# Pooling q by TensorE accumulation in the first batch of an attention and MoE kernel

## The chip, the cores and the metric

The kernel runs on one core of one Trainium2 chip. A core has five engines that work side by side, each on its own stream of instructions: TensorE (PE: matrix products; PEld in the profile is its loading of the stationary operand), VectorE (DVE), ScalarE (ACT), GpSimd (POOL) and SyncE (SP), which here only issues transfers between the main memory and the core's own memory. The metric is the time of one execution on the device, in microseconds (us); less is better.

## The reference

The inputs are q, k and v with 8 batches, 8 heads, 576 tokens and 64 numbers per head, and the weights of a MoE-like layer. Cut to what matters:

```python
q_d = q.reshape(B, H, Sd, 4, D).mean(axis=3)      # Sd = 576 / 4 = 144, k_d and v_d likewise
out_up = np.repeat(sm_attn(q_d, k_d, v_d), 4, axis=2)
scores = np.where(mask, scale * np.matmul(q, k.transpose(0, 1, 3, 2)), -1e9)   # |i - j| < 4
attn_out = out_up + np.matmul(softmax(scores), v)
h = x @ w_in                                       # x: attn_out as 4608 x 512; w_in: 512 x 2048
g = (a0 + a1*h + a2*h**2 + a3*h**3) / (1 + |b0|*|h| + |b1|*h**2 + 1e-6)
return g @ w_out                                   # w_out: 2048 x 512
```

Each head thus has two attentions: a local one in a band of 7 tokens, and a pooled one in which groups of four tokens have been averaged in q, k and v. The pooled scores are 144 x 144 for each head.

## The kernel before

**Pairs.** Two heads form a pair (class `Pair`), one head on the partitions 0 to 63 and one on 64 to 127 (j = 0 and 1). A batch has four pairs. A pair has a slot (class `Slot`) with its tiles: `qk` holds q and k for both heads, 64 numbers along the partitions, tokens along the rows (`s.qk.ap[:, 0]` is q, `[:, 1]` is k, each with 3 columns of padding ahead); `pq` holds the pooled q (`[:, 0]`) and pooled k (`[:, 1]`), 144 columns each. Batch 0 has four slots of its own, two of which lie in memory that weights need later; the later batches share slots 0 and 1.

**One pair's work.** `scores` (L427) forms the local scores in ten windows, after a mask has been put down (L417). `softmax_local` takes maxima on VectorE (L459), scales them (L466), and exponentiates on ScalarE (L474), with an accumulator read for the sums behind each exponential. `pool_qk` (L405) sums groups of four tokens of q and k on VectorE. `scores_pooled` (L444) forms the pooled scores for two pairs at a time: for each of NQ = 3 row blocks of 64 rows (blocks start 48 apart), each pair and each j one product, with 64 columns of pooled q as the stationary operand and the 144 columns of pooled k streaming. The output position alternates with the pair (`c.pos(j)`), so that the four products of a row block fall on the four different 64 x 64 quarters of the array. `softmax_pooled` takes the maxima (L489), scales them (L494) and exponentiates (L500). `normalize` (L511 to L535), `turned` (transposes L548 and L555, copies L561 to L572), `weighted_pooled` (L594) and `weighted_local` (L582), and `put_x` (L623) finish the pair into x.

**Batch 0** is the loop near L857: pairs 0 and 1 form its first group, pairs 2 and 3 its second. It runs before any MoE work can begin. There q and k are loaded once and pooled on VectorE. For the other batches `load_pooled` lets transfers that add in the memory (issued by GpSimd, L394) do the pooling, `pool_qk` is not called, and the pooled tiles come ready.

**The MoE part** goes over blocks of 512 rows of x. `h_part` forms h: the first block in plain fp32 (L718), the others in three products of split parts (L730). `middle` computes g on ScalarE (L743) and VectorE (L758 to L776), `o_part` forms the output (L795). The weights come as fp32 words and are split on ScalarE and VectorE (L338 to L361) while the first batch and block run. Batch 1 is computed beside the first block, and so on.

**The order.** Every step is given to `plan.add` with an engine, an estimated duration in us, what it reads and what it writes. `Plan.run` simulates the engines with these durations, takes at each moment the ready task with the earliest due time, and so fixes one order for each engine; the instructions are issued in that order and each engine goes through its own without overtaking. Where the plan leaves TensorE idle ahead of the first MoE work, `warm` puts in small dummy products (L929), in number 0.6 of the planned gap divided by 0.107 us. Waits between engines follow from what tasks read and write.

Of the kernel before, what the change touches and what calls it, by code (L numbers as in the profile page):

```python
# [14 lines left out]
ALU = mybir.AluOpType  # L15
AX = mybir.AxisListType.X

B, H, S, D = 8, 8, 576, 64
# [6 lines left out]
POOL = 4  # L25
SD = S // POOL
KC = SD // 2
NQ, QC = 3, SD // 3
# [5 lines left out]
PADL = 3  # L34
# [42 lines left out]
class Plan:  # L77
# [11 lines left out]
    def add(self, engine, dur, fn, reads=(), writes=(), due=None, lag=None):  # L89
        t = Task()  # L90
        t.engine, t.dur, t.fn, t.due, t.n = engine, dur, fn, due, len(self.tasks)
        t.lag, t.preds, t.succs, t.late, t.start = lag, {}, [], 1e9, None
        rk = set().union(*(r.keys for r in reads)) if reads else set()
        wk = set().union(*(w.keys for w in writes)) if writes else set()
        for k in rk | wk:
            w = self.writer.get(k)
            if w is not None:
                t.preds[w] = True
        for k in wk:
            for r in self.readers.get(k, ()):  # L100
                t.preds.setdefault(r, False)
            self.writer[k] = t
            self.readers[k] = []
        for k in rk - wk:
            self.readers[k].append(t) if k in self.readers else self.readers.__setitem__(k, [t])
        t.preds.pop(t, None)
        for p in t.preds:
            p.succs.append(t)
        self.tasks.append(t)
        return t  # L110
# [75 lines left out]
def attention_moe(  # L186
# [12 lines left out]
    nc = tc.nc  # L199
# [3 lines left out]
    add = plan.add  # L203
# [5 lines left out]
    def put(name, shape, dtype, at=None):  # L209
        nonlocal top  # L210
        offset = top if at is None else at
        n = 2 if dtype == BF16 else 4
        for d in shape[1:]:
            n *= d
        if at is None:
            top = -(-(offset + n) // 32) * 32
        ap = nc.alloc_sbuf_tensor_at(name, shape, dtype, offset=offset).ap()
        room = Room(ap, (("S", k) for k in range(offset // 32, -(-(offset + n) // 32))))
        room.at = offset
        room.size = n  # L220
        return room
# [7 lines left out]
    def flat(t):  # L229
        return t.rearrange("p a b -> p (a b)")  # L230

    high, low, bits = [], [], [[], []]
    for name, parts in (("wh", high), ("wl", low)):
        for w in range(2):
            parts.append([])
            for f in range(NFC):
                t = put(f"{name}{w}_{f}", [P, NCC, P], F32R)
# [159 lines left out]
                    (dst,), (dst,), lag=4.0,  # L397
                )

    def pool_qk(c):  # L400
        s = c.slot
        groups = s.qk.ap[:, :, PADL : PADL + S].rearrange("p t (s r) -> p t s r", r=POOL)
        add(
            "DVE", 1.28,
            lambda: nc.vector.tensor_reduce(out=s.pq.ap, in_=groups, axis=AX, op=ALU.add),  # L405
            (s.qk,), (s.pq,),
        )

    def scores(c, bk):

        s = c.slot

        def issue():
            for g in range(2):
                for j in range(2):
                    js = slice(j * D, (j + 1) * D)
                    nc.tensor.matmul(  # L417
                        bk[j].ap[g * D : (g + 1) * D, : NW // 2 * D],
                        lhsT=identb.ap[js, js], rhs=maskb.ap[js, g, :],
                        start=True, stop=False, skip_group_check=True,  # L420
                    )
            for w in range(0, NW, 2):
                for j in range(2):
                    js = slice(j * D, (j + 1) * D)
                    for g in range(2):
                        o = (w + g) * WQ
                        nc.tensor.matmul(  # L427
                            bk[j].ap[g * D : (g + 1) * D, w // 2 * D : (w // 2 + 1) * D],
                            lhsT=s.qk.ap[js, 0, PADL + o : PADL + o + D],
                            rhs=s.qk.ap[js, 1, o : o + D],  # L430
                            start=False, stop=True, skip_group_check=True,
                        )

        add("PE", 1.0, issue, (s.qk, identb, maskb), bk)

    def scores_pooled(cs, bk):
        def issue():
            for i in range(NQ):
                for c, x in zip(cs, bk):
                    pq = flat(c.slot.pq.ap)  # L440
                    for j in range(2):
                        js = slice(j * D, (j + 1) * D)
                        o = c.pos(j) * D
                        nc.tensor.matmul(  # L444
                            x.ap[o : o + D, i * SD : (i + 1) * SD],
                            lhsT=pq[js, i * QC : i * QC + D],
                            rhs=pq[js, SD:],
                            start=True, stop=True, skip_group_check=True,
                        )

        add("PE", 0.9, issue, [c.slot.pq for c in cs], bk)

    def softmax_local(c, bk):
        s = c.slot
        nm, sm = s.nm.ap, s.sm.ap
        view = two(bk)[:, :, : NW // 2 * D].rearrange("p j (c k) -> p j c k", k=D)
        add(
            "DVE", 0.74,
            lambda: nc.vector.tensor_reduce(  # L459
                out=nm[:, :NW].rearrange("p (j c) -> p j c", j=2), in_=view, axis=AX, op=ALU.max, negate=True  # L460
            ),
            bk, (s.nm,),
        )
        add(
            "DVE", 0.115,
            lambda: nc.vector.tensor_tensor(  # L466
                out=nm[:, :NW], in0=nm[:, :NW], in1=scales.ap[:, :NW], op=ALU.mult
            ),
            (s.nm, scales), (s.nm,),
        )  # L470

        def exps(j):
            for k in range(NW // 2):
                nc.scalar.activation(  # L474
                    out=s.el.ap[:, k, c.pos(j), :], in_=view[:, j, k, :], func=AF.Exp,
                    bias=nm[:, 5 * j + k : 5 * j + k + 1], scale=scale,
                    accum_out=sm[:, 2 * k + c.pos(j) : 2 * k + c.pos(j) + 1],
                )

        for j in range(2):  # L480
            add("ACT", 1.45, lambda j=j: exps(j), (bk[j], s.nm), (s.el, s.sm))

    def softmax_pooled(c, x):
        s = c.slot
        nm, sm = s.nm.ap[:, NW:13], s.sm.ap
        view = x.ap[:, : NQ * SD].rearrange("p (c k) -> p c k", k=SD)
        add(
            "DVE", 0.52,
            lambda: nc.vector.tensor_reduce(out=nm, in_=view, axis=AX, op=ALU.max, negate=True),  # L489
            (x,), (s.nm,),  # L490
        )
        add(
            "DVE", 0.115,
            lambda: nc.vector.tensor_tensor(out=nm, in0=nm, in1=scales.ap[:, NW:13], op=ALU.mult),  # L494
            (s.nm, scales), (s.nm,),
        )

        def exps():
            for i in range(NQ):
                nc.scalar.activation(  # L500
                    out=s.ep.ap[:, i, :], in_=view[:, i, :], func=AF.Exp,
                    bias=nm[:, i : i + 1], scale=scale / 16.0,
                    accum_out=sm[:, NW + i : NW + i + 1],
                )

        add("ACT", 1.07, exps, (x, s.nm), (s.ep, s.sm))
# [125 lines left out]
    def weighted_pooled(c, y):  # L632

        add("PE", 1.1, lambda: pooled_sums(c, y), (c.slot.ept, *vf), (y,))
        keep_up(c, y)
# [219 lines left out]
    bk = banks  # L855
    for q in range(2):
        cs = c0[2 * q : 2 * q + 2]  # L857
        for i, c in enumerate(cs):
            scores(c, bk[2 * i : 2 * i + 2])
            softmax_local(c, bk[2 * i : 2 * i + 2])  # L860
        for c in cs:
            pool_qk(c)
        sp = bk[4:6] if q == 0 else bk[0:2]
        scores_pooled(cs, sp)
        for c, y in zip(cs, sp):
            softmax_pooled(c, y)
        for i, c in enumerate(cs):
            normalize(c)
            (tp, t0, t1), (x, y) = FIRST[2 * q + i]
            turned(c, [bk[tp], bk[t0], bk[t1]])  # L870
            weighted_pooled(c, bk[y])
            weighted_local(c, bk[x], bk[y], due0 - 10.0 * (1 - q))
# [26 lines left out]
    for n in range(NS + LAG):  # L899
        if n < NS:  # L900
            k, s = steps[n]
# [8 lines left out]
        o = n - LAG  # L910
        if o >= 0:
            k, s = steps[o]
# [21 lines left out]
    for t in pe:  # L934
        n = int(WARM * (t.start - end) / 0.107)
# [88 lines left out]
```

## Time and profile before

| | us |
|---|---|
| three runs, median (lowest to highest) | 976.98 (975.13 to 977.01) |
| the profiled execution | 976.34 |
| its span, first to last instruction | 974.5 |
| TensorE busy in the span | 961.0 |
| VectorE busy | 833.1 |
| ScalarE busy | 810.5 |
| GpSimd busy | 147.4 |

A row of the profile names a line of the kernel, the engine and operation, the tile written and the tiles read, the shapes, and how often it occurred (x24). An engine is called busy while an instruction of it is open; TensorE's products overlap each other, so that the sum of their durations exceeds the time they took together. An entry in square brackets is the idle time of the engine just before, and what ended it. Stage tables give the same by stretches of time, counted from the start of the span. The granted clock is the share of TensorE's full clock that it was allowed. The DMA share is the mean busy share of the 16 transfer engines.

### The profile page before, as it was taken

To read this page: it belongs to the slowest core of one execution; us is meant where nothing else is said; L and a number is where in the kernel's file an instruction comes from. 1 tells how busy PE (TensorE), PEld (TensorE's weight loads), DVE (VectorE), ACT (ScalarE), POOL (GpSimd) and SP (SyncE) were. 2 spreads that over 40 slices of the span, in tenths; PEclk is the share of its full clock that TensorE was granted. 3 is DMA by queue.
4 is the path that set the end of the run, shared out by engine and by line. 5 is a ranking of instruction groups with operands and counts; after the bars stand their busy time and mean duration, and the time that the engine had idled before them with its cause. 6 is when DMAs were issued, how large, how long until landed. Compare 5 with 4: busy or idle time off the path is not lost.

```text
span 974.5 us, 19826 instructions
## 1 busy us (share of the span) xinstructions
PE 961.0 (99%) x7389; PEld 759.9 (78%) x7389; DVE 833.1 (85%) x1472; ACT 810.5 (83%) x2078; POOL 147.4 (15%) x176
## 2 busy tenths in 40 slices
PE   7999999999999999999999999999999999999997
PEld 5666657887887879987878878878788887998885
DVE  6899999998878888878788787878887888888886
ACT  6899998988789887679787979788988988867775
POOL 1121312030302121002221121203130220000000
PEclk9999999999999999999999999999999999999999
DMA  9974644252423342014333343324242320100001
GB/s 314 311 236 143 155 127 99 77 89 69 83 94 56 96 73 73 1 48 75 83 75 90 80 75 85 85 76 90 72 85 82 69 49 2 44 1 23 1 1 43
DMA packets 46359, 83.43 MB, mean 86 GB/s; under 512 B 6552, under 2 KB 29080, under 8 KB 46264
## 3 DMA queue, kind: packets, MB, share of 16 engines
q1 hardware_dynamic: 25912, 63.00, 19.6%
q0 software_dynamic: 20352, 19.19, 14.2%
q8 instruction: 58, 0.95, 0.4%
q14 instruction: 37, 0.30, 0.1%
HBM read 72.72 MB, written 9.44 MB: 84 GB/s over the span
## 4 chain that ended last, share of the span: by engine, by line
PE 86%; DVE 6%; ACT 4%; DMA 2%; issue 1%; ACTq 0%; SPq 0%; DVEq 0%
PE psum L795 38%; PE psum L730 37%; PE psum L582 3%; DMA qk<-in_qk_dram 2%; PE psum L594 2%; PE psum L548 2%; PE psum L555 2%; ACT m L743 2%; PE psum L427 1%; PE psum L444 1%; ACT el L474 1%; PE psum L718 1%; DVE m L770 1%; DVE g L767 1%; PE psum L417 1%
## 5 line engine op out<-in xcount | busy, mean ns | idle before, releaser
L795 PE MATMUL psum<-wh,g 128*128 128x512 f32 x1152 | 371.0, 403 | 0.8 <-DVE g L776 0.8
L730 PE MATMUL psum<-xs,wh 128*128 128x512 f32 (+1 forms) x1152 | 263.6, 367 | 0.0
L743 ACT ACTIVATE m<-psum,cf 128x512 f32<-128x512 f32 x288 | 215.4, 753 | 44.9 <-PE psum L730 43.3
L795 PEld LDWEIGHTS psum<-wh,g 128*128 128x128 f32 x1152 | 208.6, 188 | 50.6 <-issue 5.5
L730 PEld LDWEIGHTS psum<-xs,wh 128*128 128x128 f32 x1152 | 201.1, 188 | 37.6 <-ACT gb L743 1.0
L795 PE MATMUL psum<-wl,g 128*128 128x512 f32 x576 | 224.8, 391 | 0.0
L743 ACT ACTIVATE gb<-psum,cf 128x512 f32<-128x512 f32 x144 | 115.0, 799 | 57.5 <-PE psum L795 57.5
L767 DVE TENSOR_TENSOR g<-m,m 128x512 fp32r<-128x512 f32 x144 | 99.2, 689 | 57.1 <-ACT m L743 54.7
L394 POOL DMA_DIRECT2D pq<-in_qkp_dram x84 | 74.4, 929 | 478.2 <-DMA pq<-in_qkp_dram 436.2
L730 PE MATMUL psum<-xs,wl 128*128 128x512 f32 (+1 forms) x576 | 143.8, 371 | 0.0
L795 PEld LDWEIGHTS psum<-wl,g 128*128 128x128 f32 x576 | 108.3, 188 | 23.9
L764 DVE TENSOR_TENSOR m<-m,gb 128x512 f32<-128x512 f32 x144 | 99.0, 687 | 28.4 <-ACT gb L743 25.3
L730 PEld LDWEIGHTS psum<-xs,wl 128*128 128x128 f32 x576 | 99.6, 189 | 16.8
L474 ACT ACTIVATE el<-psum,nm 128x64 f32<-128x64 f32 x320 | 96.7, 346 | 16.0 <-DVE nm L466 16.0
L758 DVE SCALAR_TENSOR_TENSOR m<-m,cf,m 128x512 f32<-128x512 f32 x144 | 107.4, 746 | 0.3 <-ACT m L743 0.2
L743 ACT ACTIVATE gb<-m,cf 128x512 f32<-128x512 f32 x144 | 106.6, 740 | 1.1 <-DVE m L758 1.1
L770 DVE SCALAR_TENSOR_TENSOR m<-m,g 128x512 f32<-128x512 f32 x144 | 99.3, 690 | 3.1
L775 DVE TENSOR_TENSOR m<-m,m 128x512 f32<-128x512 f32 x144 | 99.2, 689 | 2.2
L776 DVE TENSOR_TENSOR g<-m,m 128x512 fp32r<-128x512 f32 x144 | 98.3, 683 | 0.8
L763 DVE TENSOR_TENSOR m<-m,m 128x512 f32<-128x512 f32 x144 | 98.5, 684 | 0.0
L743 ACT ACTIVATE m<-gb 128x512 f32<-128x512 f32 x144 | 93.5, 649 | 5.1 <-DVE m L763 2.7
L394 POOL DMA_DIRECT2D vp<-in_vp_dram x84 | 71.8, 902 | 156.2 <-DMA vp<-in_vp_dram 148.4
(63 smaller groups left out, 987.9 us busy)
## 6 DMA issues: line engine op xcount, KB each, us to landing
qk<-in_qk_dram SPq DMA_DIRECT2D x32, 590.0 KB
pq<-in_qkp_dram POOLq DMA_DIRECT2D x84, 144.0 KB, 3.4
vw<-in_vw_dram SPq DMA_DIRECT2D x32, 320.0 KB
out_dram<-xf SPq DMA_DIRECT2D x32, 256.0 KB
vp<-in_vp_dram POOLq DMA_DIRECT2D x84, 72.0 KB, 2.9
sx<-in_w_in_dram SPq DMA_DIRECT2D x11, 512.0 KB
sx<-in_w_out_dram SPq DMA_DIRECT2D x11, 512.0 KB
pq<-in_qkp_dram SPq DMA_DIRECT2D x28, 144.0 KB
```

What stands on the lines that cost most here:

```text
L394: lambda d=dst, x=src, r=r: nc.gpsimd.dma_start(out=d.ap, in_=x[b, r, :, i], accum_op=ALU.add),
L474: nc.scalar.activation(out=s.el.ap[:, k, c.pos(j), :], in_=view[:, j, k, :], func=AF.Exp, bias=nm[:, 5 * j + k : 5 * j + k + 1], scale=sca ...
L730: nc.tensor.matmul(ph.ap[:, f * t : (f + 1) * t], lhsT=(high, low)[j][0][fc].ap[:, c, :], rhs=blk.x[i].ap[:, c, :], start=(part_ == 0 and ...
L743: add("ACT", cost, lambda: nc.scalar.activation(out=out_.ap, in_=in_, func=func, **kw), (room_in, cf, *more), (out_,))
L758: lambda: v.scalar_tensor_tensor(out=tb.ap, in0=tq.ap, scalar=b1, in1=tb.ap, op0=ALU.mult, op1=ALU.add),
L763: add("DVE", 0.61, lambda: v.tensor_tensor(out=ta.ap, in0=ta.ap, in1=tq.ap, op=ALU.mult), (ta, tq), (ta,))
L764: add("DVE", 0.61, lambda: v.tensor_tensor(out=ta.ap, in0=ta.ap, in1=u.ap, op=ALU.add), (ta, u), (ta,))
L767: add("DVE", 0.61, lambda: v.tensor_tensor(out=gh.ap, in0=ta.ap, in1=tq.ap, op=ALU.mult), (ta, tq), (gh,))
L770: lambda: v.scalar_tensor_tensor(out=tb.ap, in0=tb.ap, scalar=CONE, in1=gh.ap.bitcast(F32), op0=ALU.add, op1=ALU.mult),
L775: add("DVE", 0.61, lambda: v.tensor_tensor(out=tb.ap, in0=ta.ap, in1=tb.ap, op=ALU.subtract), (ta, tb), (tb,))
L776: add("DVE", 0.61, lambda: v.tensor_tensor(out=gl.ap, in0=tb.ap, in1=tq.ap, op=ALU.mult), (tb, tq), (gl,))
L795: nc.tensor.matmul(ob[sub].ap, lhsT=g[i].ap[:, f0 : f0 + P], rhs=flat((high, low)[j][1][fc].ap), start=(fc == 0 and m == 0), stop=(fc == N ...
```

## The change

In batch 0 VectorE sums groups of four of k alone; the step is renamed `pool_k`, and its planned duration goes from 1.28 to 0.68 us. The pooled q is no longer formed. `scores_pooled` takes q as it is: for a row block it reads, as four stationary operands, the columns of q at every fourth token, starting at the first, second, third and fourth of the group, multiplies each with the pooled k, and adds the four products in the same accumulator (start at the first, stop at the last). The innermost loop runs over these four, so that all four of one quarter follow each other before the next quarter's. For batch 0 the planned duration goes from 0.9 to 3.6 us, and the step now also reads the slots' `qk`. The other batches issue what they issued before.

```diff
-    def pool_qk(c):
+    def pool_k(c):
         s = c.slot
-        groups = s.qk.ap[:, :, PADL : PADL + S].rearrange("p t (s r) -> p t s r", r=POOL)
-        add(
-            "DVE", 1.28,
-            lambda: nc.vector.tensor_reduce(out=s.pq.ap, in_=groups, axis=AX, op=ALU.add),
+        groups = s.qk.ap[:, 1, PADL : PADL + S].rearrange("p (s r) -> p s r", r=POOL)
+        add(
+            "DVE", 0.68,
+            lambda: nc.vector.tensor_reduce(out=s.pq.ap[:, 1, :], in_=groups, axis=AX, op=ALU.add),
             (s.qk,), (s.pq,),
         )
...
                         o = c.pos(j) * D
-                        nc.tensor.matmul(
-                            x.ap[o : o + D, i * SD : (i + 1) * SD],
-                            lhsT=pq[js, i * QC : i * QC + D],
-                            rhs=pq[js, SD:],
-                            start=True, stop=True, skip_group_check=True,
-                        )
-
-        add("PE", 0.9, issue, [c.slot.pq for c in cs], bk)
+
+                        if c.b == 0:
+                            at = [PADL + POOL * i * QC + r for r in range(POOL)]
+                            ls = [flat(c.slot.qk.ap)[js, a : a + POOL * (D - 1) + 1 : POOL] for a in at]
+                        else:
+                            ls = [pq[js, i * QC : i * QC + D]]
+                        for n, l in enumerate(ls):
+                            nc.tensor.matmul(
+                                x.ap[o : o + D, i * SD : (i + 1) * SD],
+                                lhsT=l,
+                                rhs=pq[js, SD:],
+                                start=(n == 0), stop=(n == len(ls) - 1), skip_group_check=True,
+                            )
+
+        add("PE", 3.6 if cs[0].b == 0 else 0.9, issue, [c.slot.pq for c in cs] + [c.slot.qk for c in cs if c.b == 0], bk)
...
         for c in cs:
-            pool_qk(c)
+            pool_k(c)
```

## The prediction, made before the changed kernel ran

> **What bounds the kernel now.** I read the table of stages first (stretch, length, busy time of PE, weight loads, VectorE, ScalarE and GpSimd with instruction counts, granted clock, DMA share, GB/s).
>
> ```profile
> 0.00:10.00 10.00, 6.93 (x83) 5.14 (x83) 2.67 (x6) 1.74 (x4) 2.28 (x8) 1.00 0.80 242
> 10.00:20.00 10.00, 7.94 (x160) 5.51 (x160) 8.50 (x17) 10.00 (x66) 0.23 (x1) 1.00 1.04 348
> 20.00:30.00 10.00, 8.74 (x143) 6.69 (x137) 8.93 (x21) 9.46 (x49) 0.00 (x0) 1.00 1.03 399
> 60.00:80.00 20.00, 20.00 (x70) 12.92 (x70) 19.76 (x35) 19.94 (x43) 2.53 (x3) 1.00 0.51 145
> 140.00:160.00 20.00, 18.32 (x163) 13.18 (x162) 18.89 (x38) 17.93 (x43) 7.60 (x9) 0.91 0.50 80
> 300.00:900.00 600.00, 600.00 (x4638) 492.69 (x4637) 505.30 (x883) 498.86 (x1252) 92.44 (x108) 1.00 0.29 64
> ```
>
> The reader is to see three regimes. From 300 us on TensorE never rests, so the end is set by when that dense work begins. Between 60 and 80 us TensorE, VectorE and ScalarE are all full. Only the first 30 us have holes, and the change lies there. TensorE is idle for 1.68 us once more, between 140 and 160 us, at a clock of 0.91.
>
> Then the chain that ended last, in order of time (start, length, what), where it crosses batch 0:
>
> ```profile
> 19.76 0.95 DVE pq L405
> ...
> 25.76 1.10 ACT ep L500 x6
> ...
> 28.12 0.74 PE psum L548 x6
> ...
> 41.38 1.72 PE psum L718 x4
> ```
>
> The last of the four qk loads has landed and its pooling begins at 19.76. VectorE, then ScalarE carry the chain to 28.12; from there TensorE does, through the first MoE products (L718). So the question is: **does the change move the 28.12?** A shift there moves the first MoE step, and with it VectorE and ScalarE, which are full behind it; the 1.68 us of TensorE rest near 150 cannot swallow that, because those two are late as well.
>
> **The change part by part.** First VectorE, its reductions in the timeline (start, length, engine and line, out<-in with shapes, idle time before):
>
> ```profile
> 10.31 1.35 DVE L405 TENSOR_REDUCE pq<-qk 128x288 f32<-128x1152 f32 x1 [0.87 <-DMA qk<-in_qk_dram]
> 11.58 0.81 DVE L459 TENSOR_REDUCE nm<-psum 128x10 f32<-128x640 f32 x1
> ...
> 21.03 0.81 DVE L459 TENSOR_REDUCE nm<-psum 128x10 f32<-128x640 f32 x1
> ...
> 23.50 0.60 DVE L489 TENSOR_REDUCE nm<-psum 128x3 f32<-128x432 f32 x1
> ```
>
> 1152 elements take 1.35 us and 640 take 0.81, so 1.05 ns an element; 576 elements come to 0.81 - 64 x 0.00105 = 0.74 us. Each of the four poolings loses 0.6 us, 2.4 us together, and the next instruction can start 0.08 us before its end (10.31 + 1.35 against 11.58). Almost all of it falls into VectorE's own holes: in the first 20 us it is busy 11.17. The saved time is worth something only where a reduction is waited for.
>
> Now TensorE. [...]
>
> ```profile
> 7.56 0.75 PE L427 MATMUL psum<-qk 64*64 64x64 f32 x40
> ...
> 10.33 0.81 PE L427 MATMUL psum<-qk 64*64 64x64 f32 x40
> ...
> 11.40 1.28 PE L444 MATMUL psum<-pq 64*64 64x144 f32 x24
> ...
> 13.90 0.81 PE L427 MATMUL psum<-qk 64*64 64x64 f32 x40 [0.21 <-DMA qk<-in_qk_dram]
> ...
> 19.78 0.81 PE L427 MATMUL psum<-qk 64*64 64x64 f32 x40 [0.60 <-DMA qk<-in_qk_dram]
> 20.52 0.50 PE L929 MATMUL psum<-maskb,identb 128*128 128x256 bf16 x3
> 20.96 1.26 PE L444 MATMUL psum<-pq 64*64 64x144 f32 x24
> 22.15 0.48 PE L548 MATMUL psum<-ident,ep 112*72 112x112 f32 x3
> 22.46 2.24 PE L929 MATMUL psum<-maskb,identb 128*128 128x256 bf16 x19
> 24.63 0.71 PE L594 MATMUL psum<-ept,vf 72*64 72x144 f32 x8
> 25.81 0.71 PE L594 MATMUL psum<-ept,vf 72*64 72x144 f32 x8 [0.47 <-ACT ept L561]
> 26.45 0.33 PE L555 MATMUL psum<-ident,el 128*128 128x128 f32 x1
> ```
>
> The source issues 12 products in each L444 group and the row counts 24: an fp32 product is two passes. A pass of 512 columns takes 1.72 / 4 = 0.43 us (L718, chain above), 0.84 ns a column; so 144 columns take 0.121 us and 64 columns 0.054 us. The new group has 48 products, 96 passes. Each works on one quarter of the array (64*64; the quarter follows from j and from the pair), and a quarter gets 24 passes.
>
> How far the quarters run beside each other is the unknown that decides. L427 answers for the old order, where the quarter changes after every product: 40 passes in a row would be 2.15 us; were each product's second pass to hold up the next product, still 20 x 0.054 = 1.08; the row shows 0.75, and a record of one pass (0.054 of streaming) lasts about 0.22, most of it its way through the array. Less that 0.22, the starts spread over 0.53 us: 10 passes, just one quarter's share. So a pass that waits for its own quarter does not hold the other three. In the new order **a quarter gets 8 passes in a row** before the next one comes, and no row has a run longer than 2. Bounds for a group: all four quarters together, 24 x 0.121 = 2.9, and 0.4 for start and end (the 1.28 row has 0.55 beside its 6 x 0.121, a wait for the second pooling among it), 3.3 us; one pass at a time, 96 x 0.121 = 11.6 + 0.4 = 12 us. L427 is the nearest row (same kind of tile, same passes), so I take **3.3 us**. Between them lies a look-ahead that ends early: overlap of two quarters, 48 x 0.121 + 0.4 = 6.2 us. That the stationary operand is now read at every fourth element appears in no row; a load that still fits under a 0.121 us pass costs nothing, one four times as long as the pass it hides in would put the group at the 12 us end again, so the bounds hold it.
>
> [...]
>
> First group, at 3.3 us. Both poolings of k are done by 10.31 + 0.74 - 0.08 = 10.97 and the second pair's scores by 11.14; the products run 11.1 to 14.4, over idle-time matmuls. The third pair's scores move from 13.90 to 14.4 and end at 15.2; its L459 follows. ScalarE hides that:
>
> ```profile
> 15.51 0.43 ACT L474 ACTIVATE el<-psum,nm 128x64 f32<-128x64 f32 x1
> ...
> 22.14 0.31 ACT L474 ACTIVATE el<-psum,nm 128x64 f32<-128x64 f32 x1 [0.33 <-DVE nm L466]
> ...
> 25.61 0.42 ACT L500 ACTIVATE ep<-psum,nm 128x144 f32<-128x144 f32 x1
> ```
>
> It was full from 10 to 20 us; it did the first pair's pooled exponentials before the second pair's last five local ones at 15.51. (Such a set takes the 1.10 us of the chain: three exponentials and three reads of their sums.) Swapped, the local ones end near 15.51 + 0.4 = 15.9, and the pooled maxima are ready at 15.2 (14.4, one L489 of 0.60, 0.2 for the scaling and the waits). Cover left: 0.7 us, so the group may take 4.0. A longer one leaves ScalarE idle.
>
> Second group. The pooling frees VectorE at 20.4 instead of 21.03, the scores at 20.59, and with 0.1 us allowed for the signal L459 starts at 20.69 instead of 21.03, **0.34 us earlier**. ScalarE's L474 moves to 21.80 and would reach L500 at 25.27 instead of 25.61. L500 also needs the pooled products: 20.6 + 3.3 = 23.9, then an L489 for each pair and the scaling, so 24.7 for the first, 25.4 for the second (ScalarE asks for that at 26.3). Cover 0.5 us, so 3.8 us a group cost nothing and 4.1 still reach the old 25.61. What TensorE did between 22.15 and 28 that is not idle time is 0.48, two of 0.71 and 0.33 (their ends overlap the next), and it fits into 23.9 to 27.8. So 28.12 becomes about 27.8.
>
> The added reads of qk hold each slot until the products end, 14.4 instead of about 11.6 in the first group; the next load into a slot is for batch 1, whose scores stand behind the first MoE products of the chain (41.38), and the DMA share is already 1.04 and 1.03 there. I cost it at nothing; it would cost when that load became the last to land. The planner counts 3.6 and 0.68 us and reorders what follows; with the three engines full later on I cost the order at 0, between -1.5 and +1.5.
>
> **Sum:** -0.34 us, rounded -0.3, on the profiled execution's 976.34 (span 974.5 and 1.8 around it): 976.0. That execution lies 0.64 under the median of 976.98, so I forecast 976.7.
>
> **The rivals.**
>
> *Look-ahead ends early* (6.2 us a group). For it: no run of 8 in the profile. Against: L427. First group 11.1 to 17.3; pooled maxima at 18.1 leave ScalarE 2.2 us idle; the third pair's exponentials and the transposes of the first pair move by about 2, the fourth pair's scores to some 22.5, the second group to 23.3 to 29.5, L500 from 25.61 to 30.3. Of these 4.7 us TensorE can use at most 1 for waiting transposes: 980.5 to 982. It decides from about 4.1 us a group: below that the gain still covers it, at 5 us it costs some 1.5.
>
> *One pass at a time* (12 us). First group to 23.1, fourth pair's scores near 28.5, second group 29.3 to 41.3, L500 at 42.1, 16 us late: 993. Against it: the 0.75 us row, where passes on other quarters do overtake. [...]
>
> *VectorE's time is used after all.* It is full at 60 to 80 us, and the stage from 140 to 160 has 1.68 us of rest and 0.09 x 20 = 1.8 us of lost clock. If the planner pulls weight conversions into the freed 2.4 us, that stage closes earlier by 2 to 3: 974 to 975. Against: VectorE has holes there already, so it lacks data, not time.
>
> *The change does nothing*: 977.0, inside the forecast's own range of 975.5 to 977.8.
>
> **How the numbers follow.** Forecast (with "nothing") 0.53, early look-ahead 0.24, one pass at a time 0.05, VectorE's time used 0.18. A measurement of this kernel can tell about 0.2%, 1.95 us, from no change, so faster means under 975.0, slower over 978.9. Faster: 0.15 of the last case and 0.03 of the forecast. Slower: 0.16 of the early look-ahead (group above some 5.2 us), 0.05, and 0.05 of the forecast by the reordering: 0.26. Same: 0.56. The range runs from 974.0 to 982.0; it leaves out the 12 us case and the far ends of the others.
>
> **What would show it.** L444 as two groups of 96 passes, each 3.1 to 3.6 us from first to last; L405 near 740 ns; fewer L929; L459 of the fourth pair near 20.7; L500 of the third pair near 25.3; the first L548 of six near 27.8. Wrong if L444's groups last over 4.2 us, if ScalarE shows an idle stretch before L500 ended by VectorE's L494, or if the stage at 140 to 160 us changes its rest or clock.

## The result, and the profile after

| us | before | after |
|---|---|---|
| runs side by side, median (lowest to highest) | 976.73 (975.13 to 977.01, 4 runs) | 982.42 (981.62 to 982.98, 4 runs) |
| ratio with its 95% interval | | 1.0061 [1.0049, 1.0073] |
| the profiled execution | 976.34 | 982.98 |
| its span | 974.5 | 981.2 |

The changed kernel is 5.7 us slower, well past the 0.2% that can be told from no change. The forecast of 976.7 fell, and the time lies 0.4 us above the upper end of the range.

The stage table of the profile after (start and end, length, then busy time with instruction counts of PE, weight loads, VectorE, ScalarE and GpSimd, granted clock, DMA share, GB/s):

```profile
0.00:10.00 10.00, 6.95 (x79) 5.07 (x79) 2.24 (x7) 1.52 (x3) 2.51 (x8) 1.00 0.82 254
10.00:20.00 10.00, 10.00 (x192) 9.78 (x191) 5.25 (x10) 8.04 (x48) 0.00 (x0) 1.00 1.04 345
20.00:30.00 10.00, 10.00 (x151) 9.37 (x151) 6.21 (x16) 8.75 (x50) 0.00 (x0) 1.00 0.99 383
...
60.00:80.00 20.00, 20.00 (x70) 12.97 (x69) 19.90 (x34) 19.34 (x33) 1.79 (x2) 1.00 0.51 160
...
140.00:160.00 20.00, 19.22 (x122) 11.63 (x121) 19.77 (x39) 20.00 (x57) 5.23 (x6) 1.00 0.46 86
160.00:180.00 20.00, 19.28 (x176) 15.31 (x176) 18.43 (x34) 16.31 (x32) 5.45 (x6) 0.91 0.45 121
...
300.00:900.00 600.00, 600.00 (x4658) 492.73 (x4657) 504.72 (x883) 500.62 (x1269) 92.62 (x108) 1.00 0.29 64
```

The holes of TensorE between 10 and 30 us are gone (10.00 and 10.00 busy against 7.94 and 8.74), and VectorE now has the holes (5.25 and 6.21 against 8.50 and 8.93). The bound of the stage has passed from ScalarE to TensorE. Behind it little has changed: the full stage at 60 to 80 us, the rest of TensorE (0.78 + 0.72 us between 140 and 180 us, against 1.68) and one stretch at a lower clock, which lies some us later. What is lost in the first 30 us is not made good.

TensorE's timeline after (start, length, engine and line, out<-in, shapes, count). L451 are the pooled scores (L444 before), L601 the weighted pooled products (L594 before), L555 the transposes of the pooled part (L548 before):

```profile
10.84 7.53 PE L451 MATMUL psum<-pq,qk 64*64 64x144 f32 x93
...
23.65 7.94 PE L451 MATMUL psum<-pq,qk 64*64 64x144 f32 x96
31.52 1.20 PE L601 MATMUL psum<-ept,vf 72*64 72x144 f32 x16
...
35.52 1.12 PE L555 MATMUL psum<-ident,ep 112*72 112x112 f32 x9
```

The two groups of 96 passes take 7.9 us each (the last three passes of the first stand in rows of their own up to 18.73), not 3.3. Of the nine passes at 35.52 the first three belong to an earlier pair: VectorE normalizes the third pair's exponentials from 35.21 to 35.82 (L532), so the third pair's transposes start at 35.88 instead of 28.12. The same time shows on the engines that wait for the groups. VectorE's timeline (L496 is the pooled maxima, L489 before; in brackets the idle time before, and what ended it):

```profile
9.83 0.75 DVE L405 TENSOR_REDUCE pq<-qk 128x144 f32<-128x576 f32 x1 [0.16 <-DMA qk<-in_qk_dram]
...
17.55 0.61 DVE L496 TENSOR_REDUCE nm<-psum 128x3 f32<-128x432 f32 x1 [2.30 <-PE psum L451]
...
30.41 0.61 DVE L496 TENSOR_REDUCE nm<-psum 128x3 f32<-128x432 f32 x1 [3.47 <-PE psum L451]
```

and ScalarE's (L507 is the pooled exponentials, L500 before; L612 copies what L601 made):

```profile
18.45 0.38 ACT L507 ACTIVATE ep<-psum,nm 128x144 f32<-128x144 f32 x1 [1.61 <-DVE nm L501]
...
32.77 0.29 ACT L612 ACTIVATE up<-psum 128x144 f32<-128x144 f32 x1 [3.52 <-PE psum L601]
...
33.50 0.39 ACT L507 ACTIVATE ep<-psum,nm 128x144 f32<-128x144 f32 x1
```

The pooling is as short as forecast (0.75 us). But VectorE then waits 2.30 and 3.47 us for the pooled scores, and ScalarE, which was full before, stands idle 1.61 us ahead of the first pair's pooled exponentials and 3.52 us later on. That last row names L601, not L451: L601 stands behind the second group on TensorE, so it began only at 31.52. The third pair's exponentials start at 33.50, against 25.61.

How much of this reaches the end is seen in the starts of three passes: the seventh pass of the first MoE block's fp32 products, the 65th, and the first pass of the second block. From the last of the three to the start of the kernel's last product that reads g, every trace has the same time (809.2 to 809.8 us).

| start, us | seventh | 65th | second block | timed median |
|---|---|---|---|---|
| before | 44.34 | 88.25 | 159.50 | 976.73 |
| after | 50.40 | 94.29 | 166.37 | 982.42 |

So 6.1 us are lost by the seventh pass, and they stay (6.0 at the 65th). (In these two executions 6.9 us are lost by the second block, and the spans differ by 6.7; the medians, 5.7, are the better measure, since single executions scatter, as the last section tells.)

### The profile page after: what moved, and what is told of

Read it like the earlier page. It is cut to its first block, busy times and chain, and to the rows that moved or that the text cites. A ratio compares the mean times of both kernels' runs of the same rounds, so it can differ in the third digit from the quotient of the medians.

```text
span 981.2 us, 20077 instructions
## 1 busy us (share of the span) xinstructions
PE 970.9 (99%) x7513; PEld 772.4 (79%) x7513; DVE 831.2 (85%) x1472; ACT 811.6 (83%) x2078; POOL 147.2 (15%) x176
## 4 chain that ended last, share of the span: by engine, by line
PE 95%; ACT 2%; DVE 2%; issue 0%; DMA 0%; ACTq 0%; DVEq 0%
PE psum L802 40%; PE psum L737 36%; PE psum L725 4%; PE psum L451 3%; PE psum L589 3%; PE psum L601 2%; PE psum L555 2%; PE psum L427 2%; PE psum L562 2%; PE psum L936 1%; PE psum L417 1%; ACT m L750 1%; ACT el L481 1%; ACT ep L507 0%; DMA maskb<-in_mask_dram 0%
```

## The experiments

Ratios are against runs of the kernel before on the same chip, with 95% intervals. "Runs of 8" below are eight passes in a row on one quarter of the array. Theory: in a run of 8 passes on one quarter, TensorE looks only about three passes ahead of the running one, so the next quarter begins when three passes of the present run remain (in the second group of the profile after, the runs begin 0.61 us, five passes of 0.122, apart). Rivals: the strided stationary operand, the planner's new order, and idle-time matmuls or the clock.

### The four rows outside, the quarters inside

```diff
             for i in range(NQ):
-                for c, x in zip(cs, bk):
-                    for j in range(2):
-                        for n in range(POOL):
+                for n in range(POOL):
+                    for c, x in zip(cs, bk):
+                        for j in range(2):
```

The same 48 products, the same planned costs and so the same order of steps; only the quarter now changes after every product, as in the kernel before.

> The changed kernel with the loops of the batch 0 products turned: the four rows of a group outside, pair and half inside, so that the quarter changes after every product again (runs of 2 passes instead of 8). Same products, same planned costs. Theory (the look-ahead past a waiting quarter ends after about 3 passes, and the group's length is the whole loss): each group 3.1 to 3.7 us instead of 7.5 to 7.9, L507 of the third pair near 25.5, time 976.0 to 977.2. Rival A (the planner's new order costs, whatever the products take): groups short, but time 978 to 981. Rival B (the stationary operand read at every fourth element is slow): groups stay above 5 us, time 978 to 982.

Measured: 976.42 (975.33 to 978.39, 11 runs), ratio 0.9999 [0.9991, 1.0008]. TensorE's timeline of this kernel (its pooled scores are L450, the MoE products L724):

```profile
11.08 3.25 PE L450 MATMUL psum<-pq,qk 64*64 64x144 f32 x96
...
16.73 1.07 PE L427 MATMUL psum<-qk 64*64 64x64 f32 x40 [2.26 <-issue]
...
23.34 3.23 PE L450 MATMUL psum<-pq,qk 64*64 64x144 f32 x96
...
30.51 1.13 PE L554 MATMUL psum<-ident,ep 112*72 112x112 f32 x9
```

A group takes 3.25 and 3.23 us, within 0.1 of the 3.3 forecast, and in the time no loss is left that can be told from nothing (the interval reaches 0.9 us either way). In the trace the seventh MoE pass still starts at 45.39, 1.05 us after that of before, and the second block at 159.86, 0.36 us after it; this execution had its half clock at 17.1 us, and before had it at 153.9, which the last section takes up. The pass time, the count of 96 and the strided operand were thus sized well; the length of the runs is what costs. How the two orders differ is seen in the stage table of the pooled scores alone, over 0.61 us, five passes of 0.122. The kernel after:

```profile
11.39:12.00 0.61, 0.61 (x11) 0.61 (x10) 1.00 1.17 309
```

and this one:

```profile
11.70:12.31 0.61, 0.61 (x28) 0.61 (x26) 1.00 1.07 332
```

The counts take in passes still open from the stretch before. With the quarters alternating, 28 passes are open or begin; with runs of 8, 11: eight that begin and three of the run before. The stretches were cut at the starts of runs, which lie 0.61 us apart. Eight passes begin in the time of five, so 8 / 5 = 1.6 quarters work at once.

The row at 16.73 shows a stop of TensorE of 2.26 us that no data wait explains; it is taken up in the last section.

### Runs of 24, of 4, and of 6 and 2

```diff
-            for i in range(NQ):
-                for c, x in zip(cs, bk):
-                    for j in range(2):
-                        for n in range(POOL):
+            for c, x in zip(cs, bk):
+                for j in range(2):
+                    for i in range(NQ):
+                        for n in range(POOL):
```

> The changed kernel with the quarter outside everything: 24 passes of a quarter in a row. Theory (a run of L passes lets the next quarter begin after L - 3 of them): (3 x 21 + 24) x 0.122 + 0.4 = 11.0 us a group, time 985 to 990. Rival (half of the runs overlap whatever their length, as 5 of 8 might also be read): (3 x 15 + 24) x 0.122 + 0.4 = 8.8 us, time 982.5 to 985.

Measured: 988.48 (987.63 to 998.43, 4 runs), ratio 1.0146 [1.0104, 1.0187]; the 998.43 came at a granted clock of 0.989, the other three at 0.998 to 1.000. TensorE's timeline:

```profile
10.76 10.50 PE L450 MATMUL psum<-pq,qk 64*64 64x144 f32 x93
...
26.54 10.92 PE L450 MATMUL psum<-pq,qk 64*64 64x144 f32 x96
```

By the look-ahead of three passes: (3 x 21 + 24) x 0.122 + 0.4 = 11.0 us; the second row shows 10.92. The rival, an overlap that is a fixed share of a run, would have given 8.8.

Then two rows of a group in one turn (runs of 4), and three rows in one turn with the fourth in another (runs of 6, then of 2):

```diff
             for i in range(NQ):
-                for c, x in zip(cs, bk):
-                    for j in range(2):
-                        for n in range(POOL):
+                for m in range(2):
+                    for c, x in zip(cs, bk):
+                        for j in range(2):
+                            for n in (2 * m, 2 * m + 1):
```

> The changed kernel with two rows of a group per turn of a quarter: runs of 4 passes. Theory (the next quarter can begin once only 3 passes of the run are left, counting the one that streams): it begins after 1 pass, so a quarter's own 24 passes set the length, 3.3 us a group, no longer than with runs of 2 (3.25). Rival (the overlap is a share of the run, 3 of 8): 4 x 5/8 = 2.5 passes a turn, 24 turns x 2.5 x 0.122 = 7.3 us, as with runs of 8.

```diff
             for i in range(NQ):
-                for c, x in zip(cs, bk):
-                    for j in range(2):
-                        for n in range(POOL):
+                for ns in ((0, 1, 2), (3,)):
+                    for c, x in zip(cs, bk):
+                        for j in range(2):
+                            for n in ns:
```

> The changed kernel with three rows of a group in one turn of the four quarters and the fourth in a second: runs of 6 and 2 passes. Theory: the next quarter begins after 3 of the 6, so a row block takes about 3 x 3 + 6 passes, less what overlaps the next turn, 12 to 15 passes: 4.4 to 5.5 us and 0.4, a group 4.7 to 5.9 us, between runs of 4 and runs of 8. Rival (share of the run): 7 us or more.

Measured: 976.06 for runs of 4 and 978.44 for 6 and 2, one run each, against a median of 975.99 (974.88 to 978.31, 23 runs) before. TensorE's timeline with runs of 4:

```profile
11.02 3.28 PE L450 MATMUL psum<-pq,qk 64*64 64x144 f32 x93
...
22.07 3.83 PE L450 MATMUL psum<-pq,qk 64*64 64x144 f32 x96
```

and with 6 and 2:

```profile
11.28 5.32 PE L450 MATMUL psum<-pq,qk 64*64 64x144 f32 x93
...
22.07 6.15 PE L450 MATMUL psum<-pq,qk 64*64 64x144 f32 x96
```

In both kernels the last three passes of the first group stand in rows of their own, so that the whole groups take 3.5 and 3.8 us with runs of 4, and 5.7 and 6.2 us with 6 and 2. The second group by length of run: 3.2 us (2), 3.8 (4), 6.2 (6 and 2), 7.9 (8), 10.9 (24). The steps are those of a look-ahead of about three passes; the same reckoning gives 3.3 us for runs of 4 and 4.7 to 5.9 for 6 and 2, and the second groups lie 0.5 and 0.25 above that, so "three" is not exact. (A fixed share of the run would have given 7.3 us for runs of 4.) The bound that the prediction gave, some 4 us a group before it costs, fits: with 3.5 to 3.8 us the seventh MoE pass starts 0.4 us later than before (44.71), with 5.7 to 6.2 it starts 2.7 us later (47.04), and the one timed run is 2.4 us slower.

### One row of the four

```diff
-                            ls = [flat(c.slot.qk.ap)[js, a : a + POOL * (D - 1) + 1 : POOL] for a in at]
+                            ls = [flat(c.slot.qk.ap)[js, a : a + POOL * (D - 1) + 1 : POOL] for a in at[:1]]
...
-        add("PE", 3.6 if cs[0].b == 0 else 0.9, issue, ...)
+        add("PE", 0.9, issue, ...)
```

Only the first row of q of each group is multiplied; the products of the other three are left out. That leaves VectorE's shorter pooling and the strided operand.

> VectorE pools k alone, and TensorE multiplies only the first of the four rows of q of each group, planned at 0.9 us as before; the products of the other three rows are left out. This is VectorE's saving and the strided stationary operand without the added passes. Theory: groups near 1.0 us, fourth pair's L459 about 0.3 us earlier than before, time 976.0 to 977.0. Rival (VectorE's freed 2.4 us are used by weight conversions and shorten the full stage up to 160 us): 973.5 to 975. Rival B (strided operand slow): groups above 1.6 us.

Measured: 978.57 (976.45 to 979.48, 10 runs), ratio 1.0022 [1.0012, 1.0031]: slower than before with less work, so what I expected of it fell. TensorE's timeline:

```profile
20.91 1.03 PE L450 MATMUL psum<-pq,qk 64*64 64x144 f32 x24
...
27.92 1.30 PE L554 MATMUL psum<-ident,ep 112*72 112x112 f32 x6 [0.79 <-DVE ep L531]
...
45.56 4.56 PE L724 MATMUL psum<-xf,wb 128*128 128x512 f32 x10
```

The 24 strided products are no slower than the plain ones (1.03 us against 1.26 before), and the chain reaches 27.92, ahead of 28.12. But six passes that took 0.74 us took 1.30, at half clock (the granted clock was 0.89 from 20 to 30 us and 0.94 from 30 to 40), and the seventh MoE pass (the first of the row at 45.56) starts 1.2 us late. In this execution the half clock accounts for that: the next six transposes, the same step as in the kernel before, come at 31.87 instead of 30.65. For the loss in the timed runs two causes were open: the clock (the planner puts in fewer idle-time matmuls, 88 against 93; that these hold the clock up was my guess, which no run had shown), or the order that it plans for a group of 0.9 and a pooling of 0.68 us. For the first:

```diff
-WARM = 0.6
+WARM = 0.95
```

> The kernel with only the first of the four rows of q multiplied (the other three products left out), with dummy products for 0.95 of the planned gaps instead of 0.6. It ran 2 us longer than before although it has less work; in its profile the granted clock was halved for 3.4 us from 27.8. Theory (fewer products before that point let the clock drop in the stretch where TensorE carries the chain): no half clock between 20 and 40 us, time 976.0 to 977.3. Rival (the planner's order, not the clock): clock full, time still 978 to 979.5.

Measured: 977.95 (976.16 to 980.72, 12 runs), ratio 1.0022 [1.0014, 1.0031]. In its trace there is no half clock between 20 and 40 us any more (the six transposes take 0.74 us, at 28.43), and the loss in the time is the same, so that stretch is not what makes it. The clock has a part all the same: the granted clock of the runs averages 0.9958 with one row (10 runs) against 0.9975 before on the same chip (20 runs), and 0.9972 against 0.9982 with more idle-time matmuls. But at one and the same clock, 0.999, the kernel with more of them took 976.16 to 977.38 us (4 runs) and the kernel before 974.88 to 976.25 (10 runs on that chip), so about 1 us remains beside it. For the second, the planned costs of before, which give VectorE, ScalarE, SyncE and GpSimd the order of the kernel before:

```diff
-            "DVE", 0.68,
+            "DVE", 1.28,
```

> VectorE pools k alone and TensorE multiplies the first of the four rows (the products of the other three left out), with the planned costs of the kernel before (1.28 and 0.9), so that VectorE, ScalarE, SyncE and GpSimd keep the order of before to the last instruction. Theory (the 2 us that the one-row kernel lost are the planner's other order, and VectorE's saving by itself is worth 0.3): 975.3 to 976.3, against before on the same chip -0.6 to 0. Rival (the strided operand or the shorter pooling itself costs): 977.5 to 979.

Measured: 976.29 (974.65 to 977.69, 11 runs), ratio 0.9997 [0.9988, 1.0005]. TensorE's timeline:

```profile
27.83 0.74 PE L554 MATMUL psum<-ident,ep 112*72 112x112 f32 x6 [0.79 <-DVE ep L531]
...
44.04 4.56 PE L724 MATMUL psum<-xf,wb 128*128 128x512 f32 x10
```

With the old order the loss is gone, so it came with the planner's order; by which way (waits, or more half clock) these runs do not part. And the 28.12 and 44.34 of before become 27.83 and 44.04: the 0.3 us that the prediction gave to VectorE's shorter pooling, no more. In the time it can't be told from nothing.

### The planner told the true cost

```diff
-        add("PE", 3.6 if cs[0].b == 0 else 0.9, issue, ...)
+        add("PE", 7.6 if cs[0].b == 0 else 0.9, issue, ...)
```

> The changed kernel with 7.6 us instead of 3.6 as the planned cost of the batch 0 products, which is what they take; only the order of the instructions and the number of dummy products changes. Theory (the products' length is the loss): groups stay 7.5 to 7.9 us, time 981 to 983.5. Rival A (a good part is the order that the planner chose on a wrong cost: products of the first pair wait behind the second group, and ScalarE waits for them from 29 to 32.8): time 977.5 to 980.5.

Measured: 986.85 (985.94 to 987.88, 4 runs), ratio 1.0109 [1.0093, 1.0126], 4.4 us worse than the change with its wrong 3.6; neither expectation held. TensorE's timeline:

```profile
24.47 0.74 PE L555 MATMUL psum<-ident,ep 112*72 112x112 f32 x6 [2.58 <-DVE ep L532]
...
27.80 8.36 PE L451 MATMUL psum<-pq,qk 64*64 64x144 f32 x96
```

The planner now puts six transpose passes of ep ahead of the second group. Their operand is late, TensorE stands for 2.58 us, idle-time matmuls follow, and the group starts at 27.80 instead of 23.65. (In this execution TensorE also had half the clock from 25.45 to 28.87; the granted clock was 0.83 from 20 to 30 us.)

### The changed work in the old order

Planned costs 1.28 and 0.9 as before, first with the quarters inside (runs of 2), then as in the change (runs of 8):

```diff
-            "DVE", 0.68,
+            "DVE", 1.28,
...
-        add("PE", 3.6 if cs[0].b == 0 else 0.9, issue, ...)
+        add("PE", 0.9, issue, ...)
```

> All four rows, quarters alternating (runs of 2 passes), planned at 1.28 and 0.9, so the order of before on the four other engines. Theory (3.3 us a group is covered, as the prediction had it): within 0.5 us of before. Rival (with the old order ScalarE asks for the pooled maxima of the first pair before its own second five exponentials, at 14.5, so the first group's 2.2 added us come out at the end): 1.5 to 2.5 us slower than before.

> The changed kernel's products (runs of 8 passes), planned at 1.28 and 0.9, so the order of before. It parts the measured +5.7 us into length and order. Theory (all of it is the length of the groups, the order gives back little): 982 to 986, no faster than the changed kernel. Rival (the order that 3.6 and 0.68 lead to is what costs): below 981.

Measured: 979.06 (978.27 to 982.07, 6 runs), ratio 1.0032 [1.0019, 1.0045], with runs of 2, and 987.46 (986.89 to 988.09, 4 runs), ratio 1.0111 [1.0096, 1.0125], with runs of 8. TensorE's timeline of the first:

```profile
16.45 0.60 PE L935 MATMUL psum<-maskb,identb 128*128 128x256 bf16 x4 [1.43 <-issue]
...
31.23 0.74 PE L554 MATMUL psum<-ident,ep 112*72 112x112 f32 x6 [0.59 <-DVE ep L531]
```

and of the second:

```profile
11.02 7.94 PE L451 MATMUL psum<-pq,qk 64*64 64x144 f32 x96
...
25.66 7.95 PE L451 MATMUL psum<-pq,qk 64*64 64x144 f32 x96
...
38.62 0.74 PE L555 MATMUL psum<-ident,ep 112*72 112x112 f32 x6 [0.59 <-DVE ep L532]
```

With runs of 8 the transposes that stood at 28.12 come at 38.62, 10.5 us late, and the kernel is 10.65 us slower (987.46 - 976.81): in the old order the 2 x 6.7 us that the groups grew come out at the end but for 2.7. The change's planned costs, 3.6 and 0.68, give 5.0 of that back (987.46 to 982.42); that the planner then puts other work between and behind the groups is the likely reason, not a shown one. With runs of 2 the old order costs 2.25 us, but its trace also has a stop of 1.43 us ahead of the third pair's scores, and this run does not tell the one from the other.

### Fewer, wider idle-time matmuls

With the quarters inside, to see whether the stop at 14 to 17 us follows the number of instructions:

```diff
-            nc.tensor.matmul(banks[7].ap[:, : 2 * P], lhsT=identb.ap, rhs=flat(maskb.ap)[:, : 2 * P], start=True, stop=True)
+            nc.tensor.matmul(banks[7].ap[:, : 4 * P], lhsT=identb.ap, rhs=flat(maskb.ap)[:, : 4 * P], start=True, stop=True)
...
-        n = int(WARM * (t.start - end) / 0.107)
+        n = int(WARM * (t.start - end) / 0.214)
```

> The kernel with quarters alternating (runs of 2), and dummy products of 512 columns in half the number, which halves the instructions TensorE fetches for them. In the run with narrow ones TensorE stood still for 2.3 us before the third pair's scores while a block of 16 KB of its instructions was on its way. Theory (it ran out of instructions): the stop of 2.3 us goes or moves, the third pair's scores start near 14.5 instead of 16.7, time 974.5 to 976.3. Rival (it waited for data, or the stop lies beside the path): the stop stays, or goes with the time at 976.0 to 977.0.

Measured: 976.01 (975.49 to 977.32, 11 runs), ratio 1.0000 [0.9991, 1.0009]. The stop stayed; it moved back in the program. TensorE's timeline:

```profile
14.15 0.31 PE L417 MATMUL psum<-maskb,identb 64*64 64x320 bf16 x4
14.29 0.51 PE L427 MATMUL psum<-qk 64*64 64x64 f32 x18
16.70 0.57 PE L427 MATMUL psum<-qk 64*64 64x64 f32 x22 [1.90 <-issue]
```

It now falls between the 18th and 19th pass of one step, where no operand is missing.

## Why the prediction was wrong, step by step

**The step that failed** is the size of the new group: "L427 is the nearest row (same kind of tile, same passes), so I take 3.3 us". That row has runs of 2 passes, and the change makes runs of 8. The text said so itself ("no row has a run longer than 2") and still let the row carry the forecast. The quarters do overtake, but only as far as about three passes: 3.25 us with runs of 2, 7.9 with runs of 8.

**The rival "look-ahead ends early"** was the right mechanism. Its size was off: it had two quarters at once, 6.2 us, and the trace has 1.6, 7.9 us. It put the second group at 23.3 to 29.5; it ran from 23.65 to 31.59. It put the third pair's exponentials at 30.3; they began at 33.50. Of these 3.2 us, 2.1 are the group's later end; the rest goes with the new order, which has L612, waiting for L601 behind the group, ahead of them. TensorE filled more of the wait with other work than the 1 us that the rival allowed (7.9 us late at the exponentials, 6.1 at the seventh MoE pass), and so 982.4 still lies close to its 980.5 to 982; that closeness is in part luck, since two errors offset each other.

**One pass at a time** (12 us) is refuted: 96 passes of 0.122 us would be 11.7 us, and the group took 7.9. Nor do the passes of different quarters start in the order of the program, even with runs of 8: were only the starts in order, the twelve runs of a group would still need 12 x 7 x 0.122 = 10.2 us. What overtakes here reaches about three passes (the next run begins 0.61 us after the one before it, five passes of its eight).

**Right, with their numbers:** the pooling at 0.74 (0.75); the pass at 0.121 (0.122); the count of 96; the strided operand at nothing (3.23 us a group); VectorE's part worth 0.3 us (28.12 to 27.83), with the rest of the 2.4 us in its own holes; a shift at the start of the dense work reaching the end (6.1 us at the seventh pass, 5.7 in the time); no change from 60 us on that could swallow it. That VectorE's freed time would be used was not borne out: it was busy 7.5 us of the first 20 (2.24 + 5.25), where it had been 11.2, and no later stage came earlier for it. "From 300 us on TensorE never rests" was read too far: it holds to 900 us, and of the last 74.5 us TensorE was busy 69.15; nothing in the forecast hangs on that.

**The order, costed at 0 within 1.5 us**, was mis-sized. Each kernel taken against the one before on its own chip, the same products in the old and the new order differ by 5.0 us (runs of 8: 10.65 and 5.69 slower), 2.1 us (runs of 2: 2.25 and 0.19 slower, part of it perhaps the stop) and 2.9 us the other way (one row: 0.52 faster and 2.34 slower). With the true cost planned, the order got worse by 4.4.

**The cover** of 0.7 and 0.5 us was worked out on the old order with ScalarE's steps swapped. A group of 3.3 us did cost nothing that the time shows, but under the new order, where the third pair's transposes start at 30.87 (the fourth pass of the row at 30.51) instead of 28.12 and other steps stand ahead of them. So "does the change move the 28.12?" was too narrow a question: the start of the dense products is what counts, and the planner can fill the time before it with other work.

**Left open:** why the planner's order for one row costs 2 us. In its trace the 1.2 us by the seventh MoE pass are that execution's half clock. The 65th pass is 0.9 us later still, but that is no loss: 24 pooled-score passes of batch 1 stand ahead of it there and behind it in the kernel before, where they take 0.97 us (89.20). The second block starts 2.3 us late, and a second stretch of half clock lies just ahead of it, at 157.6. How much of the timed 2 us is the clock and how much the order's waits was not found.

## What to carry to other kernels

When small products lie on different quarters of TensorE's array, let the quarter change after each product: accumulating four products of one quarter in a row cost 7.9 us where alternating them cost 3.2. Before trusting a row for the cost of new work, ask in what order its neighbours came; a rate measured with runs of 2 nearly held for runs of 4 (3.5 to 3.8 us) and not at all for runs of 8. Where a planner fixes the order from estimated costs, an estimate is part of the change: try the changed work under the old order too, since a truer estimate can also make the order worse.

## What the runs showed of the hardware

**A short look-ahead.** With runs of 8 passes, the next quarter begins 0.61 us, five passes, after the one before it; with runs of 24 the trace has the second and third run of a group 2.57 us apart (13.27 and 15.84), which is 21 passes. So about three passes of a run are left in both when the next quarter begins. The same shows at the end of the first group of the kernel after, where products of the next step (L417, L427) start ahead of the group's last three passes:

```profile
18.09 0.32 PE L417 MATMUL psum<-maskb,identb 64*64 64x320 bf16 x1
18.20 0.28 PE L451 MATMUL psum<-pq,qk 64*64 64x144 f32 x1
...
18.25 0.29 PE L427 MATMUL psum<-qk 64*64 64x64 f32 x2
18.32 0.28 PE L451 MATMUL psum<-pq,qk 64*64 64x144 f32 x1
...
18.45 0.28 PE L451 MATMUL psum<-pq,qk 64*64 64x144 f32 x1
```

**A stop of TensorE with no data missing.** In three kernels that get through their small products faster than the change does (quarters inside, runs of 4, wide idle-time matmuls), TensorE stands still for 1.8 to 2.3 us. The stage table of the first 16.2 us, which ends within the stop (PE, then weight loads, with counts), with the quarters inside:

```profile
0.00:16.20 16.20, 11.02 (x223) 8.92 (x224) 6.26 (x15) 7.48 (x41) 2.51 (x8) 1.00 0.90 265
```

and with the wide idle-time matmuls:

```profile
0.00:16.20 16.20, 11.53 (x222) 7.51 (x224) 6.08 (x14) 7.39 (x41) 2.51 (x8) 1.00 0.90 274
```

Runs of 4, and the quarters inside in the old order (a stop of 1.43 us), give 224 loads as well. So the stop comes after the same number of instructions, at different places of the program. In that time one block of instructions of 16 KB (58 such packets make 0.95 MB in the kernel before) was under way; the table of transfers from 14.0 to 16.5 us, with the quarters inside (queue and kind: packets, MB, share of the engines' time):

```profile
q8 instruction: 1, 0.02, 2.6%
```

That TensorE waits for its own instructions fits the equal counts of all four; no run took the block away, so it is not shown. Against it stands that the packet was under way only from 14.22 to 15.28, while the stop lasted to 16.73, and that the kernels before and after have such a packet every 6 to 12 us in the first 50 us (before at 14.04, 21.14, 32.46, 38.24 and 49.44) with no idle stretch of TensorE that issue ended. (That the block is TensorE's is an estimate: of the engines' instruction counts on the pages of the kernels before and after only TensorE's differ, 7389 and 7513 products with as many loads, and this queue has 58 and 59 packets.) In the first three kernels the stop lay beside the path as far as the time can tell: they took the time of before.

**A stretch of half clock that wanders.** Most traces have a stretch of about 3.4 us at half clock (3.413 us at 0.50 in those of before and after): at 153.9 us before, 161.2 after, 17.1 with the quarters inside, 27.9 and 157.6 with one row, and none with runs of 24 (leaving out one at the very end of every trace). The hole of TensorE nearest to it is another one from kernel to kernel (0.62 us up to 154.26 before, 0.72 up to 160.97 after, 2.26 up to 16.73 with the quarters inside, 0.79 up to 27.92 with one row), and what sets it off was not shown. The full clock ahead of its first occurrence lasts 10.24, 20.48, 146.77 or 153.60 us in these records, which are 3, 6, 43 and 45 times 3.413, its own length. The time goes with it: on one chip the 20 runs of before reach from 975.25 us at a granted clock of 0.999 to 978.69 at 0.993. A single run that differs from another by 1 to 2 us therefore tells little here.
